# Weights of a feed-forward layer loaded and cast by GpSimd-queue DMAs, and the start of the kernel re-ordered

## Chip, cores, metric

One core of a Trainium2 chip. The metric is the device time of one launch in microseconds (us). The kernel before takes 329.05 us, the median of 3 runs (328.51 to 329.32).

## The reference

Sliding-window attention, and a feed-forward layer (FFN) with a squared ReLU on its output. Batch 8, 8 heads, 576 positions, head width 64; 4608 tokens of width 512; hidden width 2048. All inputs and the output are fp32.

```python
scores = (q @ k.T) / 8                      # per batch and head
scores = where(|i - j| <= 32, scores, -1e9)
attn = softmax(scores);  x = attn @ v       # heads side by side: 4608 x 512
h = relu(x @ w_in)                          # w_in 512 x 2048
out = (s * h * h + b) @ w_out               # w_out 2048 x 512
```

The kernel uses `out = s * (h*h) @ w_out + b * colsum(w_out)`. The second part is one row, CVEC, which is made once and added when an output is copied out of PSUM.

## The kernel before

**Blocks and tiles.** The 4608 tokens are 36 blocks of 128. Attention goes block by block: block j needs q of its own rows, and k and v of loads j and j+1 (each load of k and v starts 32 rows above its block). The FFN goes by tiles: eight of one block, then fourteen of two.

**One block of attention.** SP loads fp32 rows of q, k and v (`load`, issued at L447 or L450). Up to load 4, k and q come "by rows of eight": a partition holds eight positions of one head, 2 KB contiguous; the others, and all of v, are read in 256-byte pieces. `cast_q`, `cast_k` and `cast_v` (through `move`, L469 to L477) make bf16 of them. TensorE turns k and q (`turn_rows8` L528, `turn_plain` L542; from block 11 on the DMA engines do it, L553), through one PSUM bank, TP, and ScalarE or VectorE copies the result out. TensorE makes the scores (L582), VectorE adds the mask and takes the extreme (L598), ScalarE exponentiates (L606), VectorE makes reciprocals (L614, L617), and P is scaled (L472 and L477; from block 4 on GpSimd alone). P is turned on TensorE in blocks 0 to 3 (L640), later by DMA (L633). AV (L662) follows, and its copy to bf16 is XT. Blocks 4 and on also need VO, a bf16 copy of halves of two v loads (`make_vo`), written by ScalarE or VectorE. Block 0 is done in two halves of four heads (`FINE`).

**One tile of FFN.** In groups that fill one PSUM bank: 16 matmuls of the first product (L752; 8 for a two-block tile), ReLU on ScalarE (L761), square on VectorE (L780) into GT; then four groups of four matmuls per block for the second product (L803), an eviction on VectorE (L812) that applies s and CVEC, and a store (L817). The second product uses banks OUTP and PTP in turn, but OUTP alone for the first two outputs (`NSOLO`).

**The weights.** `load_w` (L414): eight DMAs of SP's queue, 1 MB each, four of w_in (i0 to i3) and four of w_out (o0 to o3), as fp32 into four staging areas in the part of GT that the FFN uses last. Each is then cast to bf16 by four instructions of 128x512 (L471, L476): w_in on GpSimd, w_out on GpSimd or ScalarE. A square that writes a staging area waits for the casts that read it (`stage`). The string `FIRST` (L269) sets where in SP's queue each weight DMA stands among the first loads. The column sum of w_out, `cvec` (L684), is 16 full matmuls into OUTP, in four parts by w_out's four loads.

**Order.** Each step is a node with an engine or a choice of engines, a cost, a key and what it reads and writes. A planner (`_Plan.order`) goes through an estimated time: on the engine that is free first, it takes the ready node with the smallest key. For DMAs it keeps one running end for each queue and adds `dtime` to it. The order that comes out is then fixed for each engine; an instruction that waits at run time holds up all that stand behind it on its engine. Where the plan has a gap on TensorE, filler matmuls (L395, L398) are put in. In `attention_until` (L707) the nodes of attention are added up to the tile's block, and at first up to as many blocks as `FIRST` has bars.

Of the kernel before, what the change touches and what calls it, by code (L numbers as in the profile page):

```python
# [13 lines left out]
DM = H * D  # L14
# [236 lines left out]
def bass_sliding_window_symmetric__then__act_starrelu_kernel(  # L251
# [27 lines left out]
    NSPLIT, NWHOLE, NSOLO = 4, 0, 2  # L279
# [5 lines left out]
    def CSET(j):  # L285
        return ANY if j < 6 else ("pool",)
# [6 lines left out]

    WKEY = {"i": -LEAD + 100, "o": -LEAD + 600}

    with ExitStack() as es:
# [31 lines left out]
        CVEC = sb((128, DM), F32, "cvec")  # L328
        SCB = sb((128, 2), F32, "scb")
# [12 lines left out]
        AV = ps((128, NPAIR, 128), F32, "av")  # L342
# [3 lines left out]

        TP, PTP = halves(TPF), halves(PTPF)
# [8 lines left out]
        add("dve", lambda e: e.memset(NIL[:], 0.0), 100, K0, writes=["NIL"])  # L356
        add("dve", lambda e: e.memset(ZERO[:], 0.0), 150, K0, writes=["ZERO"])
# [34 lines left out]
        def fill(e, stage, n):  # L392
            for _ in range(n):
# [3 lines left out]
                else:  # L397
                    r = e.matmul((HT[0] if stage == "attn" else OUTP)[:, 0:256],  # L398
                                 lhsT=ONES[:, 0:128], rhs=ONES[:, :], start=True, stop=True)
# [11 lines left out]
        lastload = [None]  # L411
        wcnt = [0]

        def load_w(which, c):  # L414
            s_ = wcnt[0] % 4
            wcnt[0] += 1
            w32 = GT[:, 4 + 2 * s_:6 + 2 * s_, :, :].rearrange("p a b c -> p (a b c)").bitcast(
                F32).rearrange("p (g c) -> p g c", g=4)
            src = (w_in[:, :, 512 * c:512 * c + 512] if which == "i"
                   else w_out[:, 4 * c:4 * c + 4, :])  # L420
# [458 lines left out]
```

## Time and profile before

| | |
|---|---|
| Median of 3 runs | 329.05 us |
| Profiled execution | 328.95 us |
| Its span, first to last instruction | 327.2 us |
| TensorE busy (fillers included) | 312.7 us, 96% |
| VectorE, ScalarE, GpSimd busy | 232.8, 214.0, 182.5 us |
| First FFN matmul | 20.57 us |
| First matmul of the second product | 48.54 us |
| Issue to landing of a weight DMA | 8.7 to 13.0 us |

The profile gives one execution. Its page has the busy time of each engine, and the span in 40 slices with the busy share in tenths. Other views list the instructions in order of time (start, duration, engine, line, operation, tiles, and in brackets the idle time before it and what ended it), or the busy time of each engine in chosen stretches. A "q" behind an engine's name is its sequencer, which issues DMAs. Matmul ends are modelled, so a busy TensorE is not one at its peak.

### The profile page before, as it was taken

Reading aid. Unit: us, or ns where it says so; the run is one execution under the profiler, and the core shown is the slowest. Engines: PE = TensorE matmul, PEld = TensorE weight load, DVE = VectorE, ACT = ScalarE, POOL = GpSimd, SP = SyncE. Lnnn points to the kernel's source line nnn. Section 1 sums busy time; section 2 is a strip of 40 time slices with the busy share of each in tenths; the row PEclk is TensorE's granted clock in tenths of the full one; section 3 lists DMA queues with packets and bytes.
Section 4 is the critical chain, followed back from the end, with each engine's and each line's share of the span. In section 5 each row is a group of like instructions: output and inputs, shape, how many; then the busy total and the mean of one; then the engine's idle time right before and its main releaser. Section 6 shows DMA issues by size and latency. Waiting matters only on the chain.

```text
span 327.2 us, 10194 instructions
## 1 busy us (share of the span) xinstructions
PE 312.7 (96%) x3821; PEld 212.5 (65%) x3821; DVE 232.8 (71%) x988; ACT 214.0 (65%) x753; POOL 182.5 (56%) x394
## 2 busy tenths in 40 slices
PE   6675999999999999999999999999999999999996
PEld 4554776567767666766666666666666666666664
DVE  3459988879888878878787777777777677442432
ACT  3563896668769887867766666667777876533330
POOL 2537474897657988766655668486667453300000
PEclk9999999999999999999999999999999999999999
DMA  5999999999999999999999999999994332120011
GB/s 125 310 326 330 355 232 195 236 235 210 202 213 205 213 215 200 238 216 216 237 244 181 209 224 239 210 190 238 210 228 117 91 78 73 47 64 34 32 59 71
DMA packets 173949, 61.75 MB, mean 189 GB/s; under 512 B 163820, under 2 KB 164076, under 8 KB 173900
## 3 DMA queue, kind: packets, MB, share of 16 engines
q1 hardware_dynamic: 173612, 61.10, 88.3%
q8 instruction: 30, 0.49, 0.6%
q14 instruction: 19, 0.16, 0.2%
q10 hardware_dynamic: 288, 0.00, 0.0%
HBM read 36.70 MB, written 9.44 MB: 141 GB/s over the span
## 4 chain that ended last, share of the span: by engine, by line
PE 81%; DMA 7%; DVE 5%; SPq 4%; ACT 2%; issue 0%
PE ht L752 27%; PE outp L803 17%; PE ptp L803 16%; PE tp L752 9%; DMA q<-in_q_dram 4%; PE av L662 4%; PE sc L582 3%; DMA v<-in_v_dram 3%; PE sc L803 2%; ACT p L606 2%; PE av L803 2%; SPq L421 2%; DVE gt L780 1%; SPq L447 1%; SPq L450 1%; DVE kqn L471 1%
## 5 line engine op out<-in xcount | busy, mean ns | idle before, releaser
L472 POOL TENSOR_SCALAR p<-p,rc 128x128 bf16<-128x128 bf16 x257 | 101.8, 415 | 52.9 <-DVE rc L617 52.9
L606 ACT ACTIVATE p<-ss,mx 128x128 bf16<-128x128 f32 x288 | 111.8, 391 | 23.2 <-DVE mx L598 21.4
L752 PE MATMUL ht<-xt,win 128*128 128x256 bf16 (+1 forms) x1152 | 115.4, 249 | 0.6 <-POOL win L471 0.4
L752 PEld LDWEIGHTS ht<-xt,win 128*128 128x128 bf16 x1152 | 91.0, 98 | 23.7 <-POOL win L471 0.6
L780 DVE TENSOR_TENSOR gt<-r 128x512 bf16<-128x512 bf16 x144 | 68.5, 477 | 43.0 <-ACT r L761 42.2
L761 ACT ACTIVATE r<-ht 128x512 bf16<-128x512 f32 x112 | 66.3, 593 | 43.9 <-PE ht L752 40.3
L598 DVE CUSTOM_DVE_ANT_0 ss<-sc,mask 128x128 f32<-128x128 f32 x288 | 66.1, 282 | 18.0 <-PE sc L582 17.9
L803 PE MATMUL outp<-wout,gt 128*128 128x512 bf16 (+1 forms) x288 | 72.2, 374 | 0.0
L803 PE MATMUL ptp<-wout,gt 128*128 128x512 bf16 x240 | 61.6, 380 | 0.0
L606 ACT ACTIVATION_READ_ACCUMULATOR p<-ss,mx 128x1 f32 x288 | 54.4, 189 | 0.0
L471 POOL CAST ve<-v 128x512 bf16<-128x512 f32 x37 | 24.9, 672 | 29.1 <-PE av L662 16.6
L803 PEld LDWEIGHTS outp<-wout,gt 128*128 128x128 bf16 x288 | 26.1, 98 | 18.2
L803 PEld LDWEIGHTS ptp<-wout,gt 128*128 128x128 bf16 x240 | 22.3, 98 | 17.2
L752 PE MATMUL tp<-xt,win 128*128 128x256 bf16 x256 | 33.2, 273 | 0.0
L761 ACT ACTIVATE r<-tp 128x512 bf16<-128x512 f32 x32 | 18.9, 591 | 21.8 <-PE tp L752 20.6
L752 PEld LDWEIGHTS tp<-xt,win 128*128 128x128 bf16 x256 | 24.6, 98 | 8.8
L471 DVE CAST vo<-v 64x512 bf16<-64x512 f32 x54 | 27.1, 503 | 2.6 <-DMA v<-in_v_dram 1.8
L471 DVE CAST xt<-av 128x512 bf16<-128x512 f32 x35 | 24.0, 687 | 3.6 <-PE av L662 2.8
L598 DVE DVE_READ_ACCUMULATOR2_ANT mx<- 128x1 f32 x288 | 23.2, 81 | 0.0
L471 POOL CAST kqn<-q 128x512 bf16<-128x512 f32 x30 | 20.2, 672 | 2.9 <-DMA q<-in_q_dram 2.7
L471 POOL CAST kqn<-k 128x512 bf16<-128x512 f32 x31 | 19.0, 614 | 4.6 <-DMA k<-in_k_dram 4.5
L582 PEld LDWEIGHTS sc<-kqt 64*64 64x64 bf16 x864 | 12.1, 108 | 9.4 <-issue 6.5
(68 smaller groups left out, 228.4 us busy)
## 6 DMA issues: line engine op xcount, KB each, us to landing
out_dram<-outs SPq DMA_DIRECT2D x35, 256.0 KB, 3.4
q<-in_q_dram SPq DMA_DIRECT2D x32, 256.0 KB, 4.8
k<-in_k_dram SPq DMA_DIRECT2D x28, 256.0 KB, 4.8
v<-in_v_dram SPq DMA_DIRECT2D x28, 256.0 KB, 4.9
gt<-in_moe_w_in_dram SPq DMA_DIRECT2D x4, 1024.0 KB, 11.4
gt<-in_moe_w_out_dram SPq DMA_DIRECT2D x4, 1024.0 KB, 11.7
k<-in_k_dram SPq DMA_DIRECT2D x8, 192.0 KB, 3.8
v<-in_v_dram SPq DMA_DIRECT2D x8, 192.0 KB, 3.8
```

Of the source, the lines that this page charges most:

```text
L421: lastload[0] = add("sp", lambda e: [e.dma_start(w32, src)], 500, -LEAD - 900, writes=[("W32", s_, g) for g in range(4)], dsem=f"dw{s_}", ...
L447: return [e.dma_start(dst[r:r + n, :], src[b, :, s0:s0 + n, :].rearrange("h (c r) d -> c h (r d)", r=8)) for (b, s0, r, n) in pcs]
L471: return e.tensor_copy(dst, src)
L472: return e.tensor_scalar(dst, src, scale, 1.0, ALU.mult, ALU.mult)
L582: r = e.matmul(SC[hh][64 * u:64 * u + 64, pr, x0:x1], lhsT=KQT[kb][64 * hh:64 * hh + 64, NPAIR + pr, 64 * u:64 * u + 64], rhs=KQT[kt][64 * ...
L598: lambda e, ss=ss, x=x, y=y, pr=pr, hh=hh: e.tensor_tensor_reduce(out=SS[ss][:, x, :], in0=SC[hh][:, pr, :], in1=MASK[kind][:, :], scale=- ...
L606: lambda e, ss=ss, x=x, y=y: e.activation(P[pb][:, y, :], SS[ss][:, x, :], AF.Exp, bias=MX[mb][:, y:y + 1], scale=-1.0, accum_out=SM[mb][: ...
L662: r = e.matmul(avp[64 * hh:64 * hh + 64, pr, 64 * u:64 * u + 64], lhsT=vt[k0:k1, d0:d0 + 64], rhs=PTS[ptb][k0:k1, 2 * pr + hh, 64 * u:64 * ...
L752: r = e.matmul(hbank[:, nt * f:nt * f + nt], lhsT=WIN[:, kc, 128 * ft:128 * ft + 128], rhs=XT[:, kc, x0:x0 + nt], start=(kc == 0), stop=(k ...
L761: return e.activation(R1[rb][:, :], hbank[:, :], AF.Relu, bias=0.0, scale=1.0)
L780: return e.tensor_tensor(d, r, r, ALU.mult)
L803: r = e.matmul(op_[:, 0:cn], lhsT=GT[:, g_, fc, :], rhs=WOUT[:, fc, c0:c0 + cn], start=(fc == 0), stop=(fc == 15))
```

## The change

- `load_w` now issues its eight DMAs from GpSimd's queue. Each reads 1 MB of fp32 and writes bf16 straight into WIN or WOUT; the staging areas, the 32 casts and `stage` are gone. The first of them waits for the landing of the loads k0, q0 and k1.
- In `FIRST` the q, k and v of blocks 0 to 3 (k and v to load 4) come first, and there are five bars, not three: the nodes of five blocks of attention are added ahead of the first tile's.
- The casts of these loads are ordered as in `FIRST` (`ckey`), and which engines may do them is changed: ScalarE or VectorE for k1 and earlier and for q0, with GpSimd for k2 and q1, GpSimd alone for the later ones.
- k0 is loaded in 256-byte pieces and turned plainly; q4 too. The first turns use three PSUM banks. The turned P shares AV's bank (block 0's second half: PTP), and no longer has PTP to itself.
- The second product alternates between OUTP and PTP from the first output on.
- The column sum runs after the first output's matmuls, in bank TP: 16 matmuls of 32 columns each, in four column groups, then a high and a low bf16 part of the result, summed over the quarters by two full matmuls.
- The planner's `dtime` is 850 and 1400 for loads of 128 rows (700 and 1250 before), and 4000 for a weight DMA in its own queue (2680 before, in SP's).

```diff
-    FIRST = "k0 q0 k1 v0 v1 i0 q1 k2 v2 i1 i2 q2 k3 v3 i3 o0 q3 k4 v4 o1 o2 o3|||"
+    FIRST = "k0 q0 k1 v0 v1 q1 k2 v2 q2 k3 v3 q3 k4 v4 i0 i1 i2 i3 o0 o1 o2 o3|||||"
-    WSET = {"i": ("pool",), "o": ("act", "pool")}
+    WGATE = [("K32", 0), ("Q32", 0), ("K32", 1)]
-    ROWS8, NDIV = 5, 4
+    CKEY = 200
+    QROWS, KROWS, NDIV = range(0, 4), range(1, 5), 4
-    NSPLIT, NWHOLE, NSOLO = 4, 0, 2
+    NSPLIT, NWHOLE = 4, 0
     def CSET(j):
-        return ANY if j < 6 else ("pool",)
+        return ("act", "dve") if j < 1 else ("act", "dve", "pool") if j < 2 else ("pool",)
...
         def load_w(which, c):
-            s_ = wcnt[0] % 4
...
-            lastload[0] = add("sp", lambda e: [e.dma_start(w32, src)], 500, -LEAD - 900,
-                              writes=[("W32", s_, g) for g in range(4)], dsem=f"dw{s_}",
-                              dtime=2680, behind=lastload[0], ndesc=512)
-            for g in range(4):
-                dst = (WIN[:, g, 512 * c:512 * c + 512] if which == "i" else WOUT[:, 4 * c + g, :])
-                name = ("WIN", c, g) if which == "i" else ("WOUT", 4 * c + g)
-                cast(WSET[which], w32[:, g, :], ("W32", s_, g), dst, name,
-                     WKEY[which] + 4 * c + g)
+            if which == "i":
+                dst, src = WIN[:, :, 512 * c:512 * c + 512], w_in[:, :, 512 * c:512 * c + 512]
+            else:
+                dst, src = WOUT[:, 4 * c:4 * c + 4, :], w_out[:, 4 * c:4 * c + 4, :]
+            add("pool", lambda e: [e.dma_start(dst, src)], 1200, K0 + 200,
+                writes=[("WIN", c, g) if which == "i" else ("WOUT", 4 * c + g) for g in range(4)],
+                dsem=f"dw{which}{c}", dtime=4000, after=[gates[x] for x in WGATE])
...
+        def turn_bank(name, j):
+            b = {("k", 0): 0, ("k", 1): 1, ("q", 0): 2, ("q", 1): 1}.get((name, j), 0)
+            return ((TPF, "TP"), (HT[0], ("HT", 0)), (HT[1], ("HT", 1)))[b]
...
         def cvec():
...
+            def quarters(e):
+                for i in range(4):
+                    for c in range(4):
+                        r = e.matmul(TPF[32 * c:32 * c + 32, :], lhsT=ONES[:, 0:32],
+                                     rhs=WOUT[:, 4 * c + i, :], start=(i == 0), stop=(i == 3))
+                return r
...
+            def total(e):
+                e.matmul(TPF[:, :], lhsT=PART[:, :], rhs=CHI[:, :], start=True, stop=False)
+                return e.matmul(TPF[:, :], lhsT=PART[:, :], rhs=CLO[:, :], start=False, stop=True)
...
-                    writes=[("GT", g, ft) for g in gs for ft in range(f0, f0 + fg)] + stage)
+                    writes=[("GT", g, ft) for g in gs for ft in range(f0, f0 + fg)])
...
-                                 )[0 if ocnt[0] < NSOLO else ocnt[0] % (4 if last else 2)]
+                                 )[ocnt[0] % (4 if last else 2)]
```

More of the change, by code (lines that the diff above doesn't have):

```diff
@@ L328, in bass_sliding_window_symmetric__then__act_starrelu_kernel @@
         CVEC = sb((128, DM), F32, "cvec")
+        CHI, CLO = (sb((128, DM), BF16, nm) for nm in ("chi", "clo"))
+        PART = sb((128, 128), BF16, "part")
         SCB = sb((128, 2), F32, "scb")
@@ L397, in fill @@
                 else:
[L398 to L399 removed]
+                    r = e.matmul(OUTP[:, 0:256], lhsT=ONES[:, 0:128], rhs=ONES[:, :], start=True, stop=True)
             return r
@@ L684, in cvec @@
         def cvec():
[L685 to L696 removed]
+            def quarters(e):
[4 more added lines that the diff above has]
+                return r
+            add("pe", quarters, 1000, CKEY, reads=["ONES"] + [("WOUT", f) for f in range(16)],
+                writes=["TP"])
+            add("act", lambda e: e.copy(CHI[:, :], TPF[:, :]), 620, CKEY - 1000, reads=["TP"],
+                writes=["CHI"])
+            add("dve", lambda e: e.tensor_tensor(CLO[:, :], TPF[:, :], CHI[:, :], ALU.subtract), 690,
+                CKEY - 1000, reads=["TP", "CHI"], writes=["CLO"])
+            def total(e):
+                e.matmul(TPF[:, :], lhsT=PART[:, :], rhs=CHI[:, :], start=True, stop=False)
+                return e.matmul(TPF[:, :], lhsT=PART[:, :], rhs=CLO[:, :], start=False, stop=True)
+            add("pe", total, 440, CKEY - 1000, reads=["PART", "CHI", "CLO"], writes=["TP"])
+            add("dve", lambda e: e.tensor_scalar(CVEC[:, :], TPF[:, :], SCB[:, 1:2], None,
+                                                 ALU.mult), 750, CKEY - 1000,
+                reads=["TP", "SCB"], writes=["CVEC"])
         done = [0]
@@ L806, in s2 @@
                             return r
-                        add("pe", s2, 872 * cn / 512, key,
-                            reads=[("GT", gs[sub], fc) for fc in range(4 * pt, 4 * pt + 4)]
-                            + [("WOUT", fc) for fc in range(4 * pt, 4 * pt + 4)],
-                            writes=[ores])
+                        n = add("pe", s2, 872 * cn / 512, key,
+                                reads=[("GT", gs[sub], fc) for fc in range(4 * pt, 4 * pt + 4)]
+                                + [("WOUT", fc) for fc in range(4 * pt, 4 * pt + 4)],
+                                writes=[ores])
+                        if m == 0:
+                            n.tag = "full" if pt == 3 else "sums"
+                    if not cvec_done[0]:
+                        cvec()
+                        cvec_done[0] = True
                     add("dve", lambda e, ob=ob, op_=op_, c0=c0, cn=cn: e.scalar_tensor_tensor(
```

90 lines of the change are left out of this document (38 added, 52 removed).

## The prediction

> **What bounds the kernel now.** I read the page first (busy shares, slices), then the busy time by stretches, then TensorE's, VectorE's and the DMA queue's timelines of the first 75 us.
>
> ```profile
> PE 312.7 (96%) x3821; PEld 212.5 (65%) x3821; DVE 232.8 (71%) x988; ACT 214.0 (65%) x753; POOL 182.5 (56%) x394
> ...
> DMA  5999999999999999999999999999994332120011
> ...
> 10.00:20.00 10.00, 7.23 (x160) 5.39 (x160) 6.76 (x36) 5.92 (x22) 4.19 (x7) 1.00 1.09 349
> 20.00:30.00 10.00, 5.66 (x94) 4.34 (x92) 7.10 (x26) 5.99 (x22) 7.02 (x12) 1.00 1.10 329
> 30.00:40.00 10.00, 9.44 (x199) 7.49 (x200) 9.43 (x36) 7.47 (x25) 5.25 (x9) 1.00 1.10 319
> 40.00:50.00 10.00, 10.00 (x146) 7.12 (x145) 8.49 (x37) 8.47 (x25) 6.19 (x9) 1.00 1.00 237
> 50.00:60.00 10.00, 10.00 (x172) 7.08 (x166) 8.49 (x37) 5.98 (x23) 5.81 (x10) 1.00 0.97 198
> ```
>
> The columns of a stretch are its length, then busy us of PE, PEld, DVE, ACT and POOL, the granted clock, the DMA share and GB/s. From 50 us on TensorE is full (its row is 10.00 of 10 there, and 50.00 of 50 in each long stretch up to 250 us), at clock 1.00. So a microsecond of useful TensorE work that is late at about 55 us is a microsecond at the end, and one that is early is gained. Before 50 us TensorE waits or runs filler (L398, L395), and the DMA engines are full from about 4 to 44 us. The weights' own traffic sets much of that stretch:
>
> ```profile
> 24.39 0.86 DVE L471 CAST kqn<-q 128x512 bf16<-128x512 f32 x1 [2.83 <-DMA q<-in_q_dram]
> ...
> 46.11 1.03 PE L688 MATMUL outp<-wout,ones 128*128 128x512 bf16 x4
> ...
> 52.94 1.06 PE L752 MATMUL ht<-xt,win 128*128 128x128 bf16 x16
> 53.83 1.03 PE L803 MATMUL outp<-wout,gt 128*128 128x512 bf16 x4
> ```
>
> Block 2's q waited behind weights in SP's one queue; the last quarter of w_out's column sum (L688) is issued at 46.1; and by 54.7 TensorE has issued 12 groups of the first product and 4 of the second, five blocks' scores and four blocks' AV.
>
> **A marker for equal work.** In the changed kernel's TensorE order the new column sum, which needs all eight weight DMAs, stands behind 10 groups of the first product, 5 of the second, the scores of blocks 0 to 4 and the AV of blocks 0 to 3. That is the inventory above, less one FFN group (0.9 us) and with the sum still to do. So the old kernel stands at 53.8 us where the new one has just finished its sum. I forecast the time of that point; what follows is the same work on a full TensorE.
>
> **The change, part by part.**
>
> *DMA, the term that decides.* The bytes read do not change: 8.39 MB of weights. Rates come from stretches in which one kind of packet runs:
>
> ```profile
> 3.50:43.50 40.00, 29.93 (x553) 22.39 (x552) 28.07 (x118) 23.68 (x84) 19.73 (x31) 1.00 1.09 314
> ...
> 18.00:20.00 2.00, 1.87 (x56) 1.34 (x55) 1.55 (x8) 0.90 (x3) 0.27 (x1) 1.00 1.05 410
> ...
> 52.00:54.00 2.00, 2.00 (x25) 1.46 (x24) 2.00 (x19) 1.71 (x9) 0.99 (x2) 1.00 1.29 259
> ...
> 44.00:56.00 12.00, 12.00 (x191) 8.85 (x189) 10.55 (x42) 9.12 (x27) 6.46 (x10) 1.00 1.05 213
> ```
>
> 2 KB rows go at 410 GB/s, 256 B rows at 213 (mean of 12 us) to 259 (best); I take 235. Before the marker the new order needs: the weights, 8.39 MB at 410 = 20.5 us; eight loads by rows of eight, 2.10 MB at 410 = 5.1; k0 and v0 (192 KB) and v1 to v4, 1.44 MB at 235 = 6.1; and k, q, v up to v8, because ScalarE's queue has the fp32-to-bf16 casts of v5, v7 and v8 (vo) ahead of the sum's eviction: twelve loads, 3.15 MB at 235 = 13.4. Together 45.1 us of full engines (43.3 at 259, 47.1 at 213). Traffic starts at 3.5 us, and I allow 1.5 us from last packet to first use. How full are the engines kept? The old kernel moved 314 x 40 = 12.6 MB in 40 us; at the same rates (8.39 MB weights, 2.3 by eights, 1.9 plain) that is 20.5 + 5.6 + 8.1 = 34.2, so 85%. Two queues can fill each other's gaps, so 100% is the other end; I take 90%, nearer to the only row there is: 50.1 us. The marker then stands at 3.5 + 50.1 + 1.5 = 55.1 (50.1 at 100%, 58.1 at 85%). The old order cast the first vo at 35.5 (it reads v4) and the next at 46.9, by when one ring had brought them in order; the new one places these casts early.
>
> *Where the new order waits.* These casts stand in fixed queues. ScalarE's cast of v5 stands ahead of the third ReLU of the first tile and of block 2's eight exponentials; VectorE has the same wait ahead of its second square, and the cast of v4 ahead of block 0's XT. v5 can be issued only after GpSimd's cast of v0, and that stands behind all eight weight DMAs. Who waits for them is TensorE: groups 3 and on of the first product, then the scores of block 3. This is inside the 55.1 as long as the rings are shared about evenly; a rival prices the rest.
>
> *The column sum.* 16 full matmuls (four groups of about 0.97, 3.5 net) and 8 fillers go; 16 of 32 columns and two full ones come. If the quarters do not overlap they cost 16 x 0.216 (a 512-column matmul of L803 goes by in 0.87/4) + 0.43 = 3.9; if four run at once, 0.86 + 0.43 = 1.3. The 24 score matmuls (2048 columns) take 0.39 where one after another would take 0.86, so 2.2 at once: 3.5/2.2 + 0.43 = 2.0. End of the sum: 57.1. Its chain (ScalarE copy 0.58, VectorE subtract 0.7, two matmuls, VectorE scale 0.7, two evictions 0.75) is about 4.6 us, beside some 6 us of TensorE work placed there: nothing; uncovered at most 1.
>
> So the start costs 57.1 - 53.8 = **+3.3** (50.1 + 2.0 - 53.8 = -1.7 to 58.1 + 2.0 - 53.8 = +6.3).
>
> *Casts taken off GpSimd and ScalarE.* 32 casts, four in 2.3 to 2.7 us, about 20 us of GpSimd. Each chunk is usable at landing and not 2.3 us later; that is in the marker already (its end is a landing). Otherwise GpSimd is off the path: nothing. Eight issues come instead; SP's issues of the same DMAs took 1.1 (least) to 4.1 us (with a full ring). I take 1.2, the free end: 8.1 (k1 landed, the gate) + 9.6 = 17.7, then v0's cast 0.6; block 0's AV ran at 18.42 before. No loss; a rival has the other end.
>
> *Small edits.* k0 in 64-element rows: 0.20 MB at 235 instead of 410, 0.4 us later; three banks for the first turns save at most the 0.2 us waits at 9.89. Both hidden, since the weights set the marker. Two output banks from the first tile: TensorE's whole idle in 60 to 70 us was 0.5; at most that.
>
> *Behind the marker.* The first 256-token tile now stands directly behind the AV of its second block, where two groups of the second product (1.75 us) stood between before: TensorE waits for VectorE's XT copy, 0.69 and its queue. I take +0.7, bounds 0 and 3 (a copy queued behind eight mask operations of 0.21 and two squares).
>
> **Sum**: +3.3 + 0.7 = +4.0. The profiled execution took 328.95 (span 327.2 and 1.75 around it), the median is 329.05: **333.0 us**, alone 327 to 338.
>
> **Rivals.**
>
> *A: the casting DMAs are cheap.* They write half the bytes. If time goes by bytes written, the weights need 10.3 us and not 20.5; the marker falls by 10.2/0.9 to 43.8, where the elementwise engines bind about equally (five blocks at the 6 to 6.6 us between scores at 57.7, 63.7 and 70.3, from 11 us on). Sum ends at 45.8: -8, with the term behind +0.7: about 322 to 326, I say 324. For it: no row shows which side of a transfer binds; against: every byte is still read from HBM, and the 410 GB/s are of reads. Chance 0.22.
>
> *B: the loads starve.* If each DMA engine takes turns, one packet of SP's ring and one of GpSimd's, a 2 KB packet takes 80 ns and a 256 B one 17, and plain loads get 18% of the time. Up to v5 the ring needs 14.6 us; 6.0 are served by 9.5 us; 3.2 by eights take 6.4; until the weights are done (21 us more) 3.8 of the plain 5.4 are served: v5 lands at about 40. ScalarE stands still from about 26 until then, and 19 us of the old pace (block 2's exponentials at 31 to the inventory at 53, less 3 us of DMA waits) lead to 59, the sum's end to 61: +7 to +8, 337. It decides once v5 is later than about 30. The Trainium skill (DMA: Bandwidth & Descriptors, "Queues, rings and completion order") says that each DMA engine goes round-robin over the queues it has work for, packet by packet; by that rule 337, or less if a packet bundles several rows; the old trace has one busy ring and cannot show it. Chance 0.23.
>
> *C: GpSimd issues slowly.* At 4.1 us each, v0's cast comes at 41, block 0's AV 23 us late, and of the old TensorE's work by then (10 us of FFN and sums) nothing is done: about 341. It decides beyond 2 us an issue. The Trainium skill (SBUF — State Buffer, "Who interferes with whom") says that GpSimd cannot write descriptors while VectorE runs a two-port copy; a VectorE cast that takes 0.43 alone took 0.86 at 24.39 beside GpSimd's, which agrees, but no run here shows it for a DMA issue. Chance 0.07.
>
> *The name does not hold.* TensorE's first FFN group still stands ahead of block 2's scores, so "five blocks ahead" orders loads, not FFN: no gain by itself, in all cases.
>
> **How the numbers follow.** Forecast 0.48, A 0.22, B 0.23, C 0.07. Within 0.3% (1 us, what a measurement of this kernel can tell from no change) 0.08 and faster 0.05 come out of the forecast's own low end; faster 0.22 + 0.05 = 0.27, slower 0.65. Range: 325 leaves out half of A, 340 leaves out C and little of B.
>
> **What would show it.** Right: the sum's matmuls start near 55 (46.1 ended it before), ScalarE idles before a vo cast, released by DMA v, the DMA share is full to beyond 50. A: weights land by 35 and the marker is before 47. B: v5 lands near 40, weights by 36. C: GpSimd's first ve cast is after 25. The forecast falls if the marker comes before 52, or if TensorE idles behind it by more than 3 us.

## The result, and the profile after

The changed kernel takes **344.36 us** (median of 4 runs, 343.93 to 344.91); the kernel before took 328.87 us in the same session. The ratio is 1.047, 95% interval 1.045 to 1.049: 15.5 us slower. The forecast was 333.0 with a range of 325 to 340, so the sign was right and the size far too small.

The page of the changed kernel (its span is 342.8 us; the lines are the engines' busy times, TensorE's granted clock and the DMA share in 40 slices of 8.6 us, the new queue, and the shares of the chain that ended last):

```profile
PE 308.6 (90%) x3753; PEld 214.6 (63%) x3798; DVE 223.5 (65%) x966; ACT 221.5 (65%) x768; POOL 174.3 (51%) x380
...
PEclk9995769999999999999999999999999999999999
DMA  6999995835999999999999999987999663230002
...
q0 software_dynamic: 4224, 4.19, 7.2%
...
PE 82%; SPq 10%; DMA 3%; DVE 2%; issue 1%; ACT 1%
```

TensorE is busy about as long as before, fillers included (308.6 us against 312.7), in a span 15.6 us longer. Slices 4 to 6 have a low clock, and slices 7 and 9 have the DMA engines at five and three tenths, where the kernel before kept them at nine from its second slice to its thirtieth. The queue q0 holds the weights: 4.19 MB as written in bf16, in 4096 packets of 1 KB and some tiny ones. The stretches of 10 us (columns as in the prediction):

```profile
10.00:20.00 10.00, 6.92 (x128) 5.14 (x127) 8.44 (x45) 6.01 (x26) 7.85 (x12) 1.00 1.19 221
20.00:30.00 10.00, 2.40 (x49) 1.63 (x46) 0.16 (x2) 2.56 (x13) 1.85 (x3) 0.73 1.20 221
30.00:40.00 10.00, 4.35 (x63) 4.24 (x64) 2.71 (x11) 2.87 (x6) 0.87 (x1) 0.58 1.22 196
40.00:50.00 10.00, 3.63 (x84) 3.00 (x81) 3.54 (x15) 3.04 (x10) 3.97 (x6) 0.76 1.07 214
50.00:60.00 10.00, 9.95 (x159) 7.94 (x158) 9.05 (x43) 8.77 (x33) 2.74 (x4) 0.90 0.61 123
```

From 20 to 50 us no engine is busy even half the time, while the DMA engines are full to 52 us (shares of 1.20 and more in the stretches of 2 us from 48 to 52; only from 44 to 46 is it 0.70). VectorE, almost idle from 20 to 30, holds the key. Its timeline (start, duration, engine, line, operation; in brackets its idle time before and what ended it), and ScalarE's:

```profile
34.69 0.42 DVE L467 CAST vo<-v 64x512 bf16<-64x512 f32 x1 [14.52 <-DMA v<-in_v_dram]
35.12 0.42 DVE L467 CAST xt<-av 128x256 bf16<-128x256 f32 x1
...
45.70 0.42 DVE L467 CAST vo<-v 64x512 bf16<-64x512 f32 x1 [7.09 <-DMA v<-in_v_dram]
```

```profile
45.70 0.61 ACT L472 CAST vo<-v 64x512 bf16<-64x512 f32 x1 [5.31 <-DMA v<-in_v_dram]
```

VectorE stands 14.52 us for load v4, for a cast (VO) that only block 4 needs, and behind that cast in its fixed order stands block 0's XT copy (35.12). Without XT no FFN matmul can start. TensorE's timeline:

```profile
35.65 3.20 PE L765 MATMUL ht<-xt,win 128*128 128x128 bf16 x32 [13.25 <-issue]
47.52 0.65 PE L587 MATMUL sc<-kqt 64*64 64x128 bf16 x24 [6.37 <-DVE kqt L467]
66.60 1.05 PE L693 MATMUL tp<-wout,ones 128*32 128x512 bf16 x16
```

The first FFN group starts at 35.65 (20.57 before), block 2's scores at 47.52 (30.84 before), the column sum at 66.60. The trace names "issue" for the idle 13.25 us; the first FFN matmuls read XT, and its copy ends at 35.54, just before they start. The sum's end, 66.60 + 1.05 = 67.65, is the marker of equal work: the kernel before stood there at 53.8. So **13.8 of the 15.5 us are lost by the marker**, and 1.7 behind it.

Is v4 late? Not against the kernel before. There VectorE casts the same load, and GpSimd v5, at about the same times, after short waits:

```profile
35.50 0.42 DVE L471 CAST vo<-v 64x512 bf16<-64x512 f32 x1 [0.26 <-DMA v<-in_v_dram]
```

```profile
46.42 1.44 POOL L471 CAST ve<-v 128x512 bf16<-128x512 f32 x1 [1.28 <-DMA v<-in_v_dram]
```

It is late against the plan that fixed the order. The landings below are from the traces (the last semaphore update of each load); the planned times are those at which `_Plan.order` of each kernel has the same load ready (us):

| Load | Planned, before | Landed, before | Planned, changed | Landed, changed |
|---|---|---|---|---|
| q3 | 27.8 | 32.8 | 16.4 | 26.2 |
| v4 | 29.7 | 35.5 | 18.6 | 34.7 |
| v5 | 41.0 | 46.4 | 22.8 | 45.7 |

None of the three lands later than in the kernel before. But the planner, which keeps one running end for each queue, reckoned with loads that go at full pace beside the weights. So it placed the cast of v4 ahead of block 0's XT, and the casts of v5 ahead of most of the first tile's work. With v4 at 18.6 us that would have held XT up by 0.4 us in the plan; with v4 at 34.7 it held it up by the 14.5 us above.

And why do the loads come so much later than planned? Counted in the trace, from 18 us to 40 us every 2 us that are free of loads by rows of eight hold 303 to 307 weight packets and 303 to 314 load packets of 256 bytes: one for one, a pair each 105 ns on each of the 16 DMA engines. A weight packet moves 2 KB of fp32, a load packet 256 B, so the plain loads got 39 GB/s (306 x 256 B in 2 us), where alone they got 213 in the kernel before. They stayed starved until the weights were nearly done, at 42 us (the last weight packet ends at 44.0), and SP, which issues in a fixed order, was itself held up meanwhile. SP's timeline:

```profile
23.48 10.92 SPq L445 DMA_DIRECT2D q<-in_q_dram  x2
34.44 3.19 SPq L445 DMA_DIRECT2D v<-in_v_dram  x1
```

Two DMAs of q held it 10.92 us, and v5 was issued only then.

### The profile page after: what moved, and what is told of

Its sections match the earlier page's. It is cut to its first block, busy times and chain, and to the rows that moved or that the text cites. A ratio compares the mean times of both kernels' runs of the same rounds, so it can differ in the third digit from the quotient of the medians.

```text
span 342.8 us, 10067 instructions
## 1 busy us (share of the span) xinstructions
PE 308.6 (90%) x3753; PEld 214.6 (63%) x3798; DVE 223.5 (65%) x966; ACT 221.5 (65%) x768; POOL 174.3 (51%) x380
## 3 DMA queue, kind: packets, MB, share of 16 engines
q0 software_dynamic: 4224, 4.19, 7.2%
## 4 chain that ended last, share of the span: by engine, by line
PE 82%; SPq 10%; DMA 3%; DVE 2%; issue 1%; ACT 1%
PE ht L765 27%; PE outp L813 17%; PE ptp L813 16%; PE tp L765 8%; SPq L445 6%; PE av L667 4%; PE sc L587 4%; SPq L442 3%; DMA v<-in_v_dram 3%; PE sc L813 2%; PE av L813 2%; PE tp L545 1%; ACT p L611 1%; DVE ss L603 1%; DVE gt L793 1%
## 5 line engine op out<-in xcount | busy, mean ns | idle before, releaser
L765 PEld LDWEIGHTS ht<-xt,win 128*128 128x128 bf16 x1152 | 93.2, 100 | 33.6 <-issue 13.3
L793 DVE TENSOR_TENSOR gt<-r 128x512 bf16<-128x512 bf16 x144 | 66.7, 464 | 44.5 <-ACT r L774 43.8
L813 PE MATMUL outp<-wout,gt 128*128 128x512 bf16 (+1 forms) x250 | 63.5, 373 | 1.5 <-issue 0.5
L813 PEld LDWEIGHTS ptp<-wout,gt 128*128 128x128 bf16 x256 | 24.1, 98 | 23.8
L813 PEld LDWEIGHTS outp<-wout,gt 128*128 128x128 bf16 x272 | 24.7, 98 | 20.7 <-issue 0.4
L467 DVE CAST vo<-v 64x512 bf16<-64x512 f32 x37 | 18.5, 501 | 22.2 <-DMA v<-in_v_dram 21.6
L467 DVE CAST xt<-av 128x512 bf16<-128x512 f32 (+1 forms) x36 | 24.4, 679 | 7.9 <-PE av L667 7.9
L467 POOL CAST kqn<-k 128x512 bf16<-128x512 f32 x34 | 22.5, 662 | 10.6 <-DMA k<-in_k_dram 10.6
L467 POOL CAST kqn<-q 128x512 bf16<-128x512 f32 x34 | 23.0, 676 | 5.4 <-DMA q<-in_q_dram 3.2
L587 PE MATMUL sc<-kqt 64*64 64x64 bf16 (+1 forms) x864 | 16.2, 206 | 6.8 <-DVE kqt L467 6.4
```

Of the source, the lines that this page charges most:

```text
L467: return e.tensor_copy(dst, src)
L587: r = e.matmul(SC[hh][64 * u:64 * u + 64, pr, x0:x1], lhsT=KQT[kb][64 * hh:64 * hh + 64, NPAIR + pr, 64 * u:64 * u + 64], rhs=KQT[kt][64 * ...
L765: r = e.matmul(hbank[:, nt * f:nt * f + nt], lhsT=WIN[:, kc, 128 * ft:128 * ft + 128], rhs=XT[:, kc, x0:x0 + nt], start=(kc == 0), stop=(k ...
L793: return e.tensor_tensor(d, r, r, ALU.mult)
L813: r = e.matmul(op_[:, 0:cn], lhsT=GT[:, g_, fc, :], rhs=WOUT[:, fc, c0:c0 + cn], start=(fc == 0), stop=(fc == 15))
```

## The experiments

All ratios, with their 95% intervals, are against the kernel before in the same session, whose medians were 329.5 to 330.2 us; a difference between two sessions is that of their ratios, times 329 us. Every edit is planned anew, so the order of other steps can move with it. Theory 1 is that of the last paragraphs: a second queue starves the loads packet by packet, and casts that wait for them stand ahead of urgent work. Rivals: the casting DMAs themselves are slow; SP is late anyway; the new column sum or the five bars cost the time.

**e1: vo behind the turns.** One step moved, and made to wait for the block's turned q: what waits for v4 and v5 stands later in its engine's order.

```diff
-                make_vo(j)
...
                 q_turn(j)
+                make_vo(j)
...
-                     akey(j) - 10, [("V32", sl)] + ([("V32", 0, "lo")] if x == 0 else []),
+                     akey(j) - 10, [("V32", sl), ("QT", (j + 1) % NKT)] + ([("V32", 0, "lo")] if x == 0 else []),
```

> The changed kernel, with each block's VO casts ordered behind the copy of that block's turned q. Theory 1 (the loads starve beside the weights, and the time is lost because casts that are not yet needed wait for them at the head of VectorE's and ScalarE's queues): VectorE's waits of 14.5 us on v4 and 7.1 us on v5 at the vo casts go, the loads land as late as before (v4 near 34, v5 near 45), the first FFN matmul moves from 35.6 to about 22, and the time falls by 6 to 10 us, to 334 to 338. Theory 2 (starved loads would hold up whatever stands in the queues, so placing does not matter): the same time within 2 us, with the wait moved to GpSimd's casts and TensorE.

338.08 us, 1.024 (1.019 to 1.029): 7.6 us less than the changed kernel. The first FFN group starts at 21.87 (35.65), the sum at 57.31 (66.60). The packets still go one for one to about 41 us, and v4 and v5 land at 33.8 and 45.2, as in the changed kernel: the gain comes of the order alone. The wait that is left is of the same kind: TensorE stands 7.46 us for the turn of k5, which lands at 40.4 and was planned for 20.0. So the early vo is a good part of the loss, not all.

**e2: half rows.** Each weight DMA in two, of 256 columns, so that a packet reads 1 KB.

```diff
-            add("pool", lambda e: [e.dma_start(dst, src)], 1200, K0 + 200,
+            add("pool", lambda e: [e.dma_start(dst[:, :, h:h + 256], src[:, :, h:h + 256]) for h in (0, 256)], 1200, K0 + 200,
...
-                dsem=f"dw{which}{c}", dtime=4000, after=[gates[x] for x in WGATE])
+                dsem=f"dw{which}{c}", ndma=2, dtime=4000, after=[gates[x] for x in WGATE])
```

> The changed kernel, with each weight DMA issued as two of half the row length, so a packet reads 1 KB and not 2 KB; the same bytes, the same order on every engine. Theory 1 (the DMA engines take one packet of each queue in turn): a plain load's 64 packets per engine each wait for half as much weight traffic; v4 lands near 27 and not 34, v5 near 36 and not 45, while the weights take longer, and the time falls by 4 to 8 us. Rival (the engines share by bytes or by time, or the weights have priority): v4 and v5 land as late as before or later, and the time is the same or, by the longer weights, up to 4 us longer.

345.33 us, 1.047 (1.044 to 1.051): no gain. The packets do as theory 1 says: about 475 of each kind in 2 us, a pair each 67 ns, and loads come sooner (VectorE gets v4 at 28.20 us instead of 34.69, v5 at 40.97 instead of 45.70). But the weights last to about 50 us, the loads behind v5 come later (v6's cast at 51.40 instead of 48.87), GpSimd's sixteen issues delay its first casts of v to 20.98 (14.89), and block 4's scores and the sum stand at 63.52 and 66.63, as in the changed kernel. The packets did as I said, and the 4 to 8 us did not come: v4 and v5 some 5 us earlier are worth nothing by themselves.

**e3: more weights.** Four more casting DMAs behind the eight (w_in once more, into a part of GT).

```diff
+            if which == "o":
+                add("pool", lambda e: [e.dma_start(GT[:, 8 + c, :, :].rearrange("p a b -> p (a b)").rearrange(
+                    "p (g f) -> p g f", g=4), w_in[:, :, 512 * c:512 * c + 512])], 1200, K0 + 300,
+                    writes=[("GT", 8 + c, f) for f in range(16)], dsem=f"dx{c}", dtime=4000,
+                    after=[gates[x] for x in WGATE])
```

> The changed kernel, with four more casting DMAs behind the eight: w_in is loaded a second time into a part of GT that the FFN uses last, and not read. Half as much weight traffic more. Theory 1 (starved as long as weight packets are in the queue, some 31 us for eight): starving lasts about 15 us longer; v4 still lands near 34, v5 near 53 to 57, and the time rises by 8 to 12 us. Rival (the loss is the placing of the weights ahead of the first casts on GpSimd, or TensorE's lower clock, and not the share of the DMA engines): up to 3 us for the longer issuing, no more.

352.33 us, 1.069 (1.065 to 1.072), 7.1 us above the changed kernel. One for one now lasts to about 54 us, and v5 comes 8.0 us later than 45.70. ScalarE's cast of it:

```profile
53.69 0.62 ACT L477 CAST vo<-v 64x512 bf16<-64x512 f32 x1 [13.26 <-DMA v<-in_v_dram]
```

Eight microseconds more of waiting for v5 are seven at the end, a little under the 8 to 12 that I had given.

**e4: three bars.**

```diff
-    FIRST = "k0 q0 k1 v0 v1 q1 k2 v2 q2 k3 v3 q3 k4 v4 i0 i1 i2 i3 o0 o1 o2 o3|||||"
+    FIRST = "k0 q0 k1 v0 v1 q1 k2 v2 q2 k3 v3 q3 k4 v4 i0 i1 i2 i3 o0 o1 o2 o3|||"
```

> The changed kernel with three bars in FIRST, so that the nodes of three blocks of attention and not five are added ahead of the first tile. If the order that five bars make costs time by itself: 2 to 6 us faster. If it is only the loads: the same within 2 us. If the order of five bars helps against the starved loads: slower, up to 10 us.

357.47 us, 1.084 (1.081 to 1.087), 12.2 worse than the changed kernel, though v4, v5 and the sum (65.57) stand as there: only three blocks of scores are ahead of the sum, not five, and TensorE lacks attention to do behind it. I had expected at most 10. Its stretches:

```profile
60.00:70.00 10.00, 8.85 (x110) 5.80 (x111) 3.54 (x8) 2.98 (x5) 0.13 (x1) 1.00 0.21 45
70.00:100.00 30.00, 24.04 (x357) 17.50 (x353) 19.73 (x100) 18.48 (x76) 13.02 (x29) 0.83 0.50 117
```

The five bars are no part of the loss; they hide some of it.

**e5: own queue.** The kernel before, with its fp32 weight DMAs issued from GpSimd; staging, casts, sum and bars as they were.

```diff
-            lastload[0] = add("sp", lambda e: [e.dma_start(w32, src)], 500, -LEAD - 900,
+            add("pool", lambda e: [e.dma_start(w32, src)], 1200, K0 + 200,
                 writes=[("W32", s_, g) for g in range(4)], dsem=f"dw{s_}",
-                              dtime=2680, behind=lastload[0], ndesc=512)
+                dtime=2680, after=[pl.writers[("K32", 1)]], ndesc=512)
```

> The kernel before, with one edit: its eight fp32 weight DMAs are issued by GpSimd instead of SyncE, so that they stand in a queue of their own beside the loads, each for a free quarter of the staging; staging, casts, column sum and the order of the blocks stay as they were. Theory 1 (the loss comes of the second queue: beside it the loads of 256-byte rows get one packet for one, whether or not the DMA casts): the first blocks' loads starve while weights move, the last of v0 to v4 lands several us later than in the kernel before, and the time is 335 to 348 us. Theory 2 (the loss comes of the casting DMAs themselves, of slow packets that cast): without casting, the loads land within 2 us of the kernel before and the time is 327 to 332 us.

348.40 us, 1.054 (1.046 to 1.061), just above my 335 to 348. No weight DMA casts here, and the loss is there. From 18 to 24 us and from 40 to 44 us, 2 us hold 175 to 190 weight packets (4 KB in this queue) and 188 to 204 load packets: one for one again, although one packet has 16 times the bytes. From VectorE's and ScalarE's timelines:

```profile
30.06 0.80 DVE L471 CAST kqn<-q 128x512 bf16<-128x512 f32 x1 [8.60 <-DMA q<-in_q_dram]
```

```profile
31.72 0.61 ACT L476 CAST vo<-v 64x512 bf16<-64x512 f32 x1 [8.77 <-DMA v<-in_v_dram]
```

These are q3 and v4, and again they are not late against the kernel before, which cast them at 33.63 and 35.50; of the loads from q1 to v6 only v3 lands later (28.8 against 25.7). What theory 1 said of the loads, "the last of v0 to v4 lands several us later", did not happen (v4 lands at 31.7, 35.5 before), though the time came within half a microsecond of its range. The planner had q3 at 14.4 and v4 at 16.3, and put their casts early; VectorE stands for q3 while block 0's second half waits for its scaling. Behind v3's cast on GpSimd stand the casts of w_in that free the staging, so w_out is late too (its last load lands at 50.4, 43.6 before). So a second queue, with the order that the planner makes for it, is enough for a loss of this size; that DMAs cast is not needed for it.

**e6: new sum.** The kernel before with the column sum of the changed kernel: its `quarters`, `total` and copies, called behind the first output's matmuls.

```diff
-                add("pe", fn, 872, -300 + c, reads=["ONES"] + [("WOUT", f) for f in range(4 * c, 4 * c + 4)],
-                    writes=[("OUTP", 0)]).tag = "full" if c == 3 else "sums"
...
+            add("pe", quarters, 1000, 200, reads=["ONES"] + [("WOUT", f) for f in range(16)],
+                writes=["TP"])
...
```

> The kernel before, with only the column sum changed: four column groups into the transposes' bank, a copy and a rest in bf16, two matmuls that total them, called behind the first output tile instead of ahead of it. Theory 1 (the sum's form is worth no more than its matmuls): about 2.5 us of TensorE less, given back in part by the bank that the turns wait for: 326 to 331 us. Theory 2 (the sum waits for all of w_out, and the turns of the next blocks wait for its bank behind it): 333 to 340 us, with a wait of TensorE of several us on the bank TP or on the cast of w_out in front of the turns.

336.52 us, 1.016 (1.008 to 1.024): slower, in the range of theory 2, but without the wait of several us that it named (TensorE waits 0.54 us on w_out ahead of the sum). The cost is in the order: the next turns into bank TP now stand behind the sum, which needs all of w_out, and no scores are issued between block 2's (30.90) and the end of the sum (50.66), where the kernel before issues block 3's at 39.3. A short operation was put where others queue behind it.

**e7: two banks.** The kernel before, with two banks from the first tile.

```diff
-    NSPLIT, NWHOLE, NSOLO = 4, 0, 2
+    NSPLIT, NWHOLE, NSOLO = 4, 0, 0
```

> The kernel before, with only the number of FFN output banks in the first two tiles changed: two, as in all later tiles, instead of one. Theory 1 (this edit is worth nothing at this place): within 1 us of the kernel before. Theory 2 (the second bank is one that the attention of the next blocks needs): 1 to 4 us slower, with longer waits of TensorE for that bank between 50 and 90 us.

329.38 us, 0.996 (0.993 to 0.999): theory 1, a gain of about 1 us at most, and no loss.

**e8: weights spread.** e1, and the weight DMAs gated on successive loads: those of w_in on k1, v1, v2 and v3, all four of w_out on v4.

```diff
-    WGATE = [("K32", 0), ("Q32", 0), ("K32", 1)]
+    WGATE = {"i0": [("K32", 0), ("Q32", 0), ("K32", 1)], "i1": [("V32", 1)], "i2": [("V32", 2)], "i3": [("V32", 3)], "o0": [("V32", 4)], "o1": [("V32", 4)], "o2": [("V32", 4)], "o3": [("V32", 4)]}
...
-                dsem=f"dw{which}{c}", dtime=4000, after=[gates[x] for x in WGATE])
+                dsem=f"dw{which}{c}", dtime=4000, after=[gates[x] for x in WGATE[which + str(c)]])
```

> The changed kernel with make_vo behind q_turn as in the run e1_late_vo, and with the weight DMAs spread over the loads: the four of w_in gated on k1 and the three loads v1, v2, v3 that follow, those of w_out all on v4, instead of all eight on k0, q0 and k1. Theory 1 (the loads of the first five blocks are held up by as many weight packets as are in flight beside them; spreading the weights lets the loads go first): v4 lands before 30 us, the scores of block 3 stand below 33 us, the weights end later, by 45 to 52 us, and the time is 331 to 338 us. Theory 2 (what counts is when the last byte of both lands, and it is the same in any order): within 2 us of e1_late_vo, 336 to 340 us. Theory 3 (w_out is now the last to land and the first products of the FFN wait for it): slower than e1_late_vo by 3 us or more.

336.54 us, 1.017 (1.011 to 1.024). Only about 2 us below e1: the time is in the ranges of theories 1 and 2, and excludes the third. Yet up to 60 us it is well ahead: v4 and v5 land at 28.5 and 34.3, and the sum stands at 50.35 us (block 3's scores at 33.84, where I had said below 33). One wait then takes the gain back. From TensorE's timeline, and GpSimd's:

```profile
66.31 0.43 PE L667 MATMUL av<-pts,ve 128*64 128x64 bf16 x8 [6.00 <-DMA pts<-p]
```

```profile
59.87 3.21 POOL L468 TENSOR_SCALAR p<-p,rc 128x128 bf16<-128x128 bf16 x8
```

Block 4's p is scaled by GpSimd alone (3.21 us), behind its casts of later loads, then turned by a DMA; TensorE waits 6.00 us.

**e9: block 4 off GpSimd.** e8, with block 4's turn on TensorE and the scaling of blocks 4 and 5 on any engine.

```diff
-    PDMA, KQDMA, AHEAD, GATE = 4, 11, 4, 6
+    PDMA, KQDMA, AHEAD, GATE = 5, 11, 4, 6
...
-    QROWS, KROWS, NDIV = range(0, 4), range(1, 5), 4
+    QROWS, KROWS, NDIV = range(0, 4), range(1, 5), 6
```

> The run e8_staged_late_vo with one thing more: block 4's turn of p goes to TensorE instead of the transposing DMA (PDMA 5), and the products p by 1/sum of blocks 4 and 5 may go to any of three engines instead of GpSimd alone (NDIV 6). In e8_staged_late_vo TensorE stood 6.0 us at 60 us for block 4's transposing DMA, behind eight products of GpSimd (3.2 us) that came behind its casts of late loads. Theory 1 (that wait is the larger part of what e8_staged_late_vo has left to lose): the time is 329 to 333 us, level with the kernel before or a little above. Theory 2 (TensorE would have waited there anyway, for other late loads): within 2 us of e8_staged_late_vo, 334.5 to 338.5 us.

332.31 us, 1.007 (1.004 to 1.010): theory 1 (329 to 333). The two numbers are worth 3.5 us here.

**e10: the control.** The kernel before with these two numbers only.

```diff
-    PDMA, KQDMA, AHEAD, GATE = 4, 11, 4, 6
-    ROWS8, NDIV = 5, 4
+    PDMA, KQDMA, AHEAD, GATE = 5, 11, 4, 6
+    ROWS8, NDIV = 5, 6
```

> A control: the kernel before, with only the two numbers that e9_staged_block4 adds (PDMA 5, NDIV 6). Theory 1 (these two help only where GpSimd and SyncE are late with block 4, which the kernel before is not): 328 to 332 us. Theory 2 (they help any kernel of this family, and what e9_staged_block4 gains is no gain of the staged weights): 324 to 327 us.

335.47 us, 1.018 (1.013 to 1.023): neither theory. They cost the kernel before 6 us, so what they gain in e9 is no gain at large. That they repair there an order which loads later than planned had broken is my reading; no run shows it by itself.

**e11: all weights behind v4.**

```diff
-    WGATE = [("K32", 0), ("Q32", 0), ("K32", 1)]
+    WGATE = [("V32", 4)]
```

> The changed kernel with one edit: all eight weight DMAs wait for v4, so that they come behind the loads of the first five blocks instead of beside them. Theory 1 (the loads are late only because weight packets are turned in between): v4 lands before 30 us instead of 34 us, the scores of blocks 2 and 3 stand before 30 us instead of 47.5 and 54 us. Then the weights stand beside v5 and the loads behind it, and those starve instead; the first FFN product stands near 29 us, and the time is 338 to 352 us, for the same packets wait in another place. Theory 2 (the loads are late because SyncE issues them late, for staging buffers and rings that it waits for whatever GpSimd does): the scores of blocks 2 and 3 stay behind 38 us.

359.37 us, 1.090 (1.088 to 1.092). Up to v5 all is as theory 1 says: without weights beside them the loads are early (v4 lands at 20.9, v5 at 26.2). From TensorE's timeline:

```profile
22.06 0.44 PE L587 MATMUL sc<-kqt 64*64 64x128 bf16 x24 [1.05 <-DVE kqt L467]
26.39 0.45 PE L587 MATMUL sc<-kqt 64*64 64x128 bf16 x24 [0.24 <-DVE kqt L467]
28.32 1.07 PE L765 MATMUL ht<-xt,win 128*128 128x128 bf16 x16 [0.40 <-DMA win<-in_moe_w_in_dram]
33.06 1.07 PE L765 MATMUL ht<-xt,win 128*128 128x128 bf16 x16
49.06 0.61 PE L545 MATMUL tp<-ident,kqn 128*128 128x128 bf16 x4 [14.94 <-DVE kqt L467]
```

Scores of blocks 2 and 3 stand at 22.06 and 26.39 (47.52 and 53.98 in the changed kernel), which excludes theory 2. Then the weights meet the loads behind v5. From 26 to 50 us each 2 us hold 297 to 310 weight packets and 297 to 320 load packets of 256 bytes, the cleanest stretch of all. ScalarE stands for v6, VectorE's square for ScalarE, the copy kqt for VectorE, TensorE for kqt, 14.94 us. ScalarE's timeline, and SP's:

```profile
46.34 0.62 ACT L472 CAST vo<-v 64x512 bf16<-64x512 f32 x1 [16.56 <-DMA v<-in_v_dram]
```

```profile
23.61 5.32 SPq L445 DMA_DIRECT2D v<-in_v_dram  x1
29.05 6.62 SPq L445 DMA_DIRECT2D k<-in_k_dram  x1
35.72 6.47 SPq L445 DMA_DIRECT2D q<-in_q_dram  x1
42.23 6.02 SPq L445 DMA_DIRECT2D v<-in_v_dram  x1
```

A plain load of 1024 packets takes 1024/154 = 6.6 us at one for one (308 in 2 us), and SP issues one load in about as long. The same starving in another place costs twice as much, 29.7 us, and more than the 352 that I had given as the end. Yet v6 lands at 46.3, where the kernel before had it at 50.4: here too it is not the landing but what stands behind the wait.

**e12: e9 without spreading.** e1 with the same two numbers.

```diff
-    PDMA, KQDMA, AHEAD, GATE = 4, 11, 4, 6
+    PDMA, KQDMA, AHEAD, GATE = 5, 11, 4, 6
...
-    QROWS, KROWS, NDIV = range(0, 4), range(1, 5), 4
+    QROWS, KROWS, NDIV = range(0, 4), range(1, 5), 6
```

> The run e1_late_vo with the two numbers of e9_staged_block4 (PDMA 5, NDIV 6) and no spreading of the weights. Theory 1 (spreading the weights is needed, since without it the loads of block 4 are themselves late): 333 to 337 us, 3 us or more above e9_staged_block4. Theory 2 (spreading is worth nothing; the order of the engines' queues is all): within 2 us of e9_staged_block4.

340.01 us, 1.031 (1.029 to 1.033), 7.7 above e9 and more than theory 1 gave (333 to 337): without spreading, the two numbers cost about 2 us (e1 had 1.024). TensorE waits 9.19 us, to 42 us, for the turn of k5 behind GpSimd's cast.

**e13, e14, e15: the old column sum** in the changed kernel, in e9 and in e8, called ahead of the first output as in the kernel before.

```diff
-            add("pe", quarters, 1000, CKEY, reads=["ONES"] + [("WOUT", f) for f in range(16)],
-                writes=["TP"])
...
+                add("pe", fn, 872, -300 + c, reads=["ONES"] + [("WOUT", f) for f in range(4 * c, 4 * c + 4)],
+                    writes=[("OUTP", 0)]).tag = "full" if c == 3 else "sums"
...
```

> The changed kernel with the column sum of the kernel before: sixteen products 128 columns wide into the first output bank, in four steps ahead of the first output, in place of the four column groups, their copy and rest and the two totals. Theory 1 (the loss is the second queue's, and the sum is worth its matmuls): 343 to 348 us, the old sum 2 to 3 us longer on TensorE but filling time in which TensorE waits for late loads anyway. Theory 2 (the new sum, which waits for all of w_out and holds the turns' bank, causes a part of the loss): 337 to 341 us.

> The run e9_staged_block4 (weights spread over the loads, make_vo behind q_turn, block 4's turn on TensorE) with the column sum of the kernel before. Theory 1 (with the loads on time, the new sum costs what e6_new_sum showed, through the bank that the turns wait for): 325 to 330 us, level with the kernel before or up to 4 us faster. Theory 2 (what e9_staged_block4 has left to lose stands elsewhere): 332 to 336 us, by the 2 to 3 us more that the old sum takes on TensorE.

> The run e8_staged_late_vo with the column sum of the kernel before, and without the two numbers for block 4. Theory 1 (the wait for block 4's transposing DMA comes of the order that the sum's keys make, and goes with it): 329 to 334 us. Theory 2 (it comes of GpSimd's late casts and stays): 336 to 340 us.

e13: 344.89 us, 1.046 (1.042 to 1.049). The new sum is no part of the changed kernel's loss. e14: **329.29 us, 0.998 (0.996 to 1.001)**, level with the kernel before, as theory 1 had it. e15: 334.50 us, 1.014 (1.011 to 1.018), between its two theories; the wait for block 4's DMA, which theory 1 said would go, is still there (4.44 us, to 65.44). The stretches of e14, where the changed kernel had 2.40, 4.35 and 3.63 us of TensorE:

```profile
20.00:30.00 10.00, 6.39 (x111) 4.99 (x109) 6.13 (x27) 5.62 (x22) 3.85 (x6) 0.84 1.24 223
30.00:40.00 10.00, 9.94 (x188) 8.61 (x187) 8.12 (x39) 6.58 (x26) 4.07 (x7) 0.88 1.26 205
40.00:50.00 10.00, 10.00 (x154) 6.74 (x157) 8.48 (x36) 8.31 (x31) 2.20 (x4) 1.00 1.14 207
```

So four changes of order and gating give the whole loss back, with the weights still cast by DMAs in a queue of their own. Each is measured on top of the last: 1.047; vo later 1.024 (7.6 us); weights spread 1.017 (2.1, not beyond its intervals); block 4 off GpSimd 1.007 (3.5); the old sum 0.998 (2.8). Taken in another order the shares would differ, as e12, e13 and e15 show. No version was found that is faster than the kernel before by more than the measurement can tell.

## Why the prediction was wrong

**TensorE is full from 50 us, so what is late there is late at the end: right for the changed kernel.** Marker +13.8, end +15.5. The term behind the marker was +0.7 (0 to 3) and measured 1.7, and the wait that it was made for is in the trace: TensorE stands 1.68 us at 121.91 for VectorE's XT copy, ahead of the first two-block tile. It is no rule for every order: in e8 the sum ends at 51.40, ahead of the kernel before, and the run still loses about 6 us, mostly by the 6.00 us wait behind it.

**The step that failed is "this is inside the 55.1": the waits in the new order were put at nothing.** The DMA term itself came out nearly right. It had all traffic up to v8, the last load needed, done by 3.5 + 50.1 = 53.6; v8 landed at 56.2. So the marker would have been near 60 (56.2 + 1.5 + 2.0) if the work ahead of it had gone on beside the traffic, as the sum took for granted. It did not: from 20 to 50 us TensorE was busy for 10.4 of 30 us (fillers included), above all because casts that block 4 needs stood ahead of block 0's copy, and after v5 came at 45.7 another 20.9 us went by until the sum. The three vo casts that I had named stood 14.5, 7.1 and 5.3 us. The worst is the one I gave half a sentence, "the cast of v4 ahead of block 0's XT". The clue stood in my own text: the old order cast v4 at 35.5, and the new one would cast it early, although my sum had no time at which v4 would land. My condition, "as long as the rings are shared about evenly", was no safeguard either: they were shared evenly by packets, and thus unevenly by bytes. The sign "DMA share full to beyond 50" came true (1.29 from 50 to 52 us) while the forecast failed, for a full DMA engine does not show which bytes it moves first. And the sign, slower, was right for another reason than the traffic that the sum gives.

How much of this is the order and how much the sharing? With the landings unchanged, the order of one step is worth 7.6 us (e1). Moving weights out of the loads' way adds 2.1 to that (e8, not beyond its intervals), and 7.7 where block 4 is off GpSimd (e12 to e9). So the two do not simply add; spreading without any change of order was not run. That the planner's separate queue ends made the order wrong follows from its own times above; a planner that shares the DMA engines between queues was not tried.

**Rival B is what happened, at +7 to +8 instead of +15.5.** Its packet-by-packet turns are what the trace shows. The Trainium skill ("DMA: Bandwidth & Descriptors", section "Queues, rings and completion order") says that each DMA engine goes round-robin over its queues, packet by packet; the trace agrees, 304 packets against 306 in 2 us. B also saw that what waits for v5 would stand still. It fell short in two terms. It had v5 at 40, and it came at 45.7: B had the weights done at about 37 us, and they ended at 44.0, since their first packet started only at 12.7 us and they lasted 31 us, not 27; and SP did not even issue v5 before 34.4. And the pace behind: 19 us from v5's landing to the sum's start, measured 20.9 (45.7 to 66.6). So B's mis-sized terms are 5.7 for v5 and 1.9 for the pace, which make its 59 to the 66.6 measured. What B did not say is that v5 at 45.7 is no later than in the kernel before (46.4); the loss needs the new order as well. Chance 0.23 was too little for a mechanism with a rule behind it and against it only that "the old trace has one busy ring".

**Rival A: refuted.** Weight packets took a median of 96 ns for 2 KB read and 1 KB written, where a packet of 2 KB that is not cast took 84 ns in the kernel before. Time does not go by the bytes written.

**Rival C: refuted.** GpSimd's timeline:

```profile
8.80 3.18 POOL L422 DMA_DIRECT2D win<-in_moe_w_in_dram  x4 [5.60 <-DMA k<-in_k_dram]
11.95 3.00 POOL L422 DMA_DIRECT2D wout<-in_moe_w_out_dram  x4
14.89 1.79 POOL L467 CAST ve<-v 128x512 bf16<-128x512 f32 x3
```

An issue is 0.75 to 0.94 us, under the 1.2 taken, and the first ve cast comes at 14.89. So all eight weight DMAs were issued by 15 us.

**The column sum.** 2.0 us predicted; 1.05 for the sixteen and 0.4 for the two totals. Its place was the cost that I did not see. Where the start is otherwise in order it loses 2.8 us (e9 to e14) to 5 (e6), for turns queue behind it (seen in e6's order, argued for e9); in the changed kernel it costs nothing (e13: 1.046 against 1.047).

**Small edits: right.** Two banks gave at most about 1 us in the kernel before (e7), near the 0.5 allowed. **"The name does not hold": wrong in its "no gain".** Without five bars the changed kernel is 12 us slower (e4).

## What to carry to other kernels

Where a fixed order is made from estimated times, a transfer that moves to a queue of its own must still share the DMA engines in the estimate. Here v4 and v5 came when they had come before, and the new plan had them 16 and 23 us sooner. So look for the steps that the plan places early on the strength of such a landing, and find what stands behind each in its engine's order: a cast for block 4 ahead of block 0's copy cost more than any transfer.

Before a second queue is used, compare packet sizes: beside it the other queue gets one packet for one, so small packets starve for as many packets as the large transfer has, however fair the bytes look. One shared queue was here a priority order, and a second one gave it up; if it must be, gate its DMAs on the loads that are wanted first, and measure, for e8 and e11 do this with 6 and 30 us of loss.

## What the runs showed of the hardware

- Two busy queues share a DMA engine one packet for one at three sizes: 256 B beside packets of 1 KB read (67 ns a pair), 2 KB (105 ns) and 4 KB (about 190 of each in 2 us, 168 ns). The trace counts and doesn't show the turns, so whether single packets or equal bundles alternate stays open.
- An engine that issues can stand for long at one DMA: SP up to 6.62 us for one load (e11). In that trace each of the four issues of 5.32 to 6.62 us ends with 2448 to 2548 pieces of 256 bytes issued and not yet begun, so a limit on what may wait in the queue (its ring) is the likely reason.
- TensorE's granted clock fell while it idled, to 0.58 from 30 to 40 us, and 32 matmuls of the first product, 1.95 us at full clock, took 3.20. From 36 to 40 us (0.71) and from 48 to 52 (0.50) TensorE was busy throughout, so by an estimate from these rows about 3 us of its time went to the clock there; how much of the 15.5 us this is was not measured by itself.
- Sixteen 512-column matmuls in four 32-column groups take 1.05 us, as long as four full ones (1.03).
